# The first pair's product placed behind the scores of all four first pairs, with GpSimd's zeros put off and another order of decoding

## The chip, the cores and the metric

One core of a Trainium2 chip runs the kernel. The metric is the device time of one execution in microseconds (us), here the median of a few runs. The core has TensorE (PE in the profile, its weight loads PEld), VectorE (DVE), ScalarE (ACT), GpSimd (POOL), and SyncE (SP), which issues the transfers. Each engine works through its own list of instructions in order, and they wait for each other by semaphores.

## The reference

Windowed attention of 8 batches, 8 heads, 576 positions and 64 dimensions, then a gated network over all 4608 tokens. Heads 0 to 3 see the last 32 positions, heads 4 to 7 every fourth of the last 128.

```python
scores = scale * np.matmul(q, k.transpose(0, 1, 3, 2))
rel = pos[:, None] - pos[None, :]
mask_plain = (rel >= 0) & (rel < 32)
mask_dil = (rel >= 0) & (rel < 32 * 4) & (rel % 4 == 0)
scores = np.where(masks[None, :, :, :], scores, -1000000000.0)
attn = np.exp(scores - np.max(scores, axis=-1, keepdims=True))
attn = attn / (np.sum(attn, axis=-1, keepdims=True) + 1e-09)
x = np.matmul(attn, v)               # tokens 4608 x 512
h = x @ w_in                         # 512 x 2048
g = h * (1.0 / (1.0 + np.exp(-1.702 * h)))
out = g @ w_out                      # 2048 x 512
```

The inputs are float64; the host only rearranges and hands over their bits.

## The kernel before

**Attention.** The work is split in 32 "pairs" of heads, four to a batch (NC = 4). The first four pairs (batch 0) run in a form of their own at the start, since nothing else can be done before they give the first 512 tokens. For each: scores (two mask products at L470 with the tile ident, then 80 small products at L482 into the PSUM tile sp, which has one buffer), softmax (VectorE's maximum L502 and subtract L349, ScalarE's exponential L506, VectorE's sum L520, the added constant L510 and the reciprocal L512, GpSimd's two multiplies L349), two VectorE transposes L529 into ct (two buffers), the product with v (L575) into first_x, and the drain of first_x: ScalarE writes the high part of x (xs, L342), VectorE subtracts for the low part (xs, L349), and the rest of the tokens is copied (L342, L344). All four products write to the one tile first_x, so each waits for the drain of the one before (the key FOUR in the plan).

**Weights.** They come as 8-byte numbers and are decoded on the core. decode(n) issues one transfer of 512 KB, two scalings on ScalarE (L394, L395), the sign (L388 on ScalarE or L390 on VectorE), a shift (L398) and an add on VectorE or GpSimd, a copy for the high part (L342, L344) and a subtract for the low part (L349). n runs over w_in and w_out in turn (wi_kept, wo_kept: 16 blocks of 128 columns or rows each). The third to fifth borrow other tiles for their bits: n = 3 borrows the tile bt. bt needs zeros in it before the attention of the next batches; GpSimd writes them (L1207).

**Network.** The tokens are done in groups of 512. Groups m0 to m2 run block by block f: up products into hp (L848, 12 for each f: three for each of four c, where c is the quarter of x that pair c gives), the gate (ScalarE L856, VectorE L857, ScalarE L342 into gh and a subtract into gl), down products into acc (L785, L786, L789). The later tokens go in three blocks p, q and r that save products by sums (L991, L1106). Every product in float32 is done as three, of high and low parts.

**What sets the order.** The class Plan. Each operation is added with costs for each engine that may do it, an urgency (lower goes first), and the keys that it reads and writes; placed() then works through time and puts the operations in an order for each engine. Up to 60 us it fills TensorE's idle time with warm-up products (idle): large ones with ident (L1237) and small ones with ones (L1241). fetched() is the planner's idea of TensorE's instruction blocks: a block ends at instruction 193 and each 256 after it, and blocks holds when the next may be used. A small warm-up counts 4 instructions, a large one 2, the scores of a pair 180, a product 184.

Of the kernel before, what the change touches and what calls it, by code (L numbers as in the profile page):

```python
# [18 lines left out]
NC = DM // P  # L19
NF = DF // P  # L20
# [13 lines left out]
QT = 5  # L34
W = 64
# [12 lines left out]
class Plan:  # L48
# [62 lines left out]
    def placed(self, warm_until, soon, late=None):  # L111
# [22 lines left out]
        def fetched(count, when, cost):  # L134

            n = issued[0]
            issued[0] += count
            for j in range(len(blocks) - 1, 1 << 30):
                edge = 193 + 256 * j
                if edge >= n + count or edge > 1500:  # L140
                    return when + cost
                part = cost * (edge - n) / count
                at = max(when + part, blocks[j])
                blocks.append(at + (6.1 if at < 18.0 else 4.2))
                when, cost, n, count = at, cost - part, edge, count - (edge - n)

        open_ = [set() for _ in free]
# [4 lines left out]
        order = []  # L152
# [64 lines left out]
def tile_windowed_attention_then_gated_mlp(  # L217
# [134 lines left out]
    cells = [area(at, 2).bitcast(U64) for at in (18, 20, 4, 0, 2)]  # L352
    words = arena[:, 6:9].bitcast(U32)

    def decode(n, urgency):


# [3 lines left out]

        f = n // 2
        if n % 2:
            src, hi, lo, key = w_out[f], wo(f)[:, 0], wo(f)[:, 1], f"wo{f}"
        else:
            src, hi, lo, key = w_in[f], wi(f)[:, 0], wi(f)[:, 1], f"wi{f}"
# [42 lines left out]
    def lots(k):  # L411

        if 0 < k < NC:
            return f"first qk{k}", f"first v{k}"
        return "qk0", "v0"
# [98 lines left out]
    def softmax(k, urgency):  # L514
# [8 lines left out]
            add({POOL: 0.85, DVE: -0.48}, urgency, lambda e, a=a: pair(  # L523
                e, pr[:, a], pr[:, a], sm[:, a, :, None].broadcast_to([P, QT, W]), ALU.mult), (SM,), (f"{PR}.{a}",))
        if k < NC:

            for a in range(2):
                to = ct.rearrange("p h t a q -> p (h t a q)")[:, a * QT * W:a * QT * W + QT * W]
                add({DVE: 0.48}, urgency, lambda e, a=a, to=to: V.transpose(  # L529
                    out=to, in_=pr[:, a].rearrange("p t w -> p (t w)")), (PR, f"{PR}.{a}"), (f"{CT}.{a}",))  # L530
            return
        for half in (0, 1):
            add({DVE: 0.42}, urgency, lambda e, half=half: V.transpose(  # L533
# [145 lines left out]
        add({DMA: 66}, urgency, lambda e: load(dst, rests_x[:, y]), [f"xr{y}{i}.{n}" for i in range(NC) for n in range(3)],  # L679
            (f"tr{b}",))  # L680

    def first_attention(k, urgency):

        load_qk(k)
        load_v(k)
        add({PE: 1.5 if k else 2.3}, urgency - 1.0e5, lambda e: scores(k), (lots(k)[0],), ("sp",), count=180)
        softmax(k, urgency)
        add({PE: 1.4}, urgency - 1.0e5, lambda e: first_product(k), (lots(k)[1], f"ct{turn(k)}.0", f"ct{turn(k)}.1"), FOUR,
            count=184)
        drain_x(k, urgency)  # L690

    def attention(k, urgency):

# [501 lines left out]
              Block("r", (B, 7), (dests[B], dests[7]), late_units)]  # L1195

    for c in range(NC):
        first_attention(c, c)
        if c in (1, 2):
            decode(c - 1, c + 1.3)  # L1200
    for b, g in enumerate(main):
        g.split_x()
        if b == 0:
            for n in range(2, 2 * NF - 8):
                decode(n, 25.0 + 2.3 * n)
            zeroed = [f"bt.{m}" for m in range(8)]
            add({POOL: 1.2}, 20.0, lambda e: G.memset(bt, 0.0), (), ("bt", "btl", *zeroed))  # L1207
            add({ACT: 0.5}, 30.0, lambda e: mask_dilated(), (), ("mask",))
        if b == 1:
            for c in range(NC):  # L1210
                attention(2 * NC + c, 2000.0 + c)
            for u in range(PAIRS):
                sum_weights(u)
                sum_out_weights(u)
        if b == 2:
            for k in range(3 * NC, INNER):
                attention(k, 1000.0 * (k // NC) + k % NC)
        for f in range(NF):
            g.up(f)
            if b == 0 and f == 2:  # L1220
                for c in range(NC):
                    attention(NC + c, 46.0 + 12.9 * c)
                for n in range(2 * NF - 8, 2 * NF):
                    decode(n, 25.0 + 2.3 * n)
# [67 lines left out]
```

## Time and profile before

| | |
|---|---|
| median of 3 runs | 829.16 us (829.06 to 829.52) |
| profiled execution: its time, its span | 828.89 us, 827.2 us |
| TensorE busy in the span | 811.2 us, 98% |
| VectorE, ScalarE, GpSimd busy | 669.7 us (81%), 515.0 us (62%), 327.8 us (40%) |
| TensorE on the chain that ended last | 88% of the span |
| warm-up products in the first 38.2 us | 11.86 us |

A row of a timeline gives start and length in us, engine, line, operation, tile written and tiles read, the array's part and the shape, how many instructions are put together, and in brackets how long the engine stood idle before it and what released it. A row of a stretch gives the busy time and number of instructions of each engine in it, and the TensorE clock that was granted (1.00 is full). A wait for "issue" is one for which the profile shows no other work.

### The profile page before, as it was taken

How to read it: one execution, taken by the hardware profiler on the slowest of the kernel's cores; microseconds unless marked ns; L12 is line 12 of the kernel's file. 1: busy time of each engine (PE TensorE's matmuls, PEld its weight loads, DVE VectorE, ACT ScalarE, POOL GpSimd, SP SyncE). 2: the span in 40 equal slices, each digit the busy share in tenths (PEclk: the TensorE clock that was granted, in tenths of full speed). 3: DMA queues.
4: the chain of work that ended last, by engine and by line, in shares of the span. 5: the costliest groups of instructions: out<-in, count | busy, mean ns of one | idle time of the engine just before them, and what ended most of it. 6: DMA issues, size and time to landing. Idle time of an engine off the chain costs nothing.

```text
span 827.2 us, 18837 instructions
## 1 busy us (share of the span) xinstructions
PE 811.2 (98%) x7240; PEld 653.5 (79%) x7240; DVE 669.7 (81%) x1104; ACT 515.0 (62%) x992; POOL 327.8 (40%) x296
## 2 busy tenths in 40 slices
PE   7899999999999999999999999999999999999997
PEld 4678777888878888878788788888888888888886
DVE  6898989787888778898989998977679876867575
ACT  7998986676676777586776655446446544544340
POOL 3343336566655663324235357331125431112251
PEclk8799999999999999999999999999999999999999
DMA  9476658889757567868878878675665658664546
GB/s 359 152 244 193 181 192 287 295 281 314 249 189 254 183 200 257 267 190 280 279 229 261 261 233 260 219 269 168 214 193 182 211 186 273 203 222 149 189 151 181
DMA packets 109610, 188.12 MB, mean 227 GB/s; under 512 B 26448, under 2 KB 55376, under 8 KB 109520
## 3 DMA queue, kind: packets, MB, share of 16 engines
q1 hardware_dynamic: 109376, 186.78, 69.3%
q8 instruction: 57, 0.93, 0.5%
q14 instruction: 33, 0.27, 0.1%
q10 hardware_dynamic: 144, 0.13, 0.0%
HBM read 140.64 MB, written 45.09 MB: 225 GB/s over the span
## 4 chain that ended last, share of the span: by engine, by line
PE 88%; DVE 7%; ACT 1%; issue 1%; DMA 1%; SPq 0%; DVEq 0%; ACTq 0%
PE hp_m L848 15%; PE up_q L991 9%; PE up_r L991 9%; PE up_p L991 8%; PE second_q_Q L1106 5%; PE second_r_Q L1106 5%; PE second_p_Q L1106 5%; PE acc_m L785 5%; PE acc_m L789 5%; PE acc_m L786 4%; PE sp L482 3%; PE second_r_Z L1106 3%; PE second_R L1106 3%; PE second_q_Z L1106 3%; PE second_p_Z L1106 2%; PE av L607 2%
## 5 line engine op out<-in xcount | busy, mean ns | idle before, releaser
L349 POOL TENSOR_TENSOR arena<-arena 128x256 f32<-128x256 f32 (+3 forms) x109 | 118.0, 1091 | 155.7 <-DVE wi_last_units L349 34.7
L848 PE MATMUL hp_m<-xs,wi_kept 128*128 128x512 f32 x504 | 129.1, 398 | 0.7 <-DVE xs L349 0.4
L848 PEld LDWEIGHTS hp_m<-xs,wi_kept 128*128 128x128 f32 x504 | 93.3, 188 | 22.5 <-DVE arena L857 1.6
L342 ACT ACTIVATE wo_kept<-arena 128x512 fp32r<-128x512 f32 x115 | 71.9, 629 | 42.3 <-PE second_r_Q L1106 11.4
L349 POOL TENSOR_TENSOR wo_kept<-arena,wo_kept 128x512 fp32r<-128x512 f32 x34 | 45.3, 1340 | 105.5 <-ACT wo_kept L342 72.2
L991 PE MATMUL up_p<-wi_kept,xs 128*128 128x512 f32 x336 | 84.7, 394 | 2.2 <-DVE arena L349 1.3
L991 PE MATMUL up_r<-wi_kept,xs 128*128 128x512 f32 x336 | 85.3, 389 | 0.0
L991 PE MATMUL up_q<-wi_kept,xs 128*128 128x512 f32 x336 | 83.4, 389 | 0.0
L991 PEld LDWEIGHTS up_p<-wi_kept,xs 128*128 128x128 f32 x336 | 62.1, 188 | 16.8 <-DVE arena L349 2.2
L991 PEld LDWEIGHTS up_q<-wi_kept,xs 128*128 128x128 f32 x336 | 63.0, 188 | 13.4 <-DVE arena L1013 0.3
L991 PEld LDWEIGHTS up_r<-wi_kept,xs 128*128 128x128 f32 x336 | 63.1, 188 | 13.1
L349 DVE TENSOR_TENSOR wo_kept<-arena,wo_kept 128x512 fp32r<-128x512 f32 x87 | 65.3, 761 | 5.9 <-ACT wo_kept L342 5.4
L349 POOL TENSOR_TENSOR wo_kept<-wi_last_units,wo_kept 128x512 fp32r<-128x512 f32 x23 | 31.9, 1388 | 84.6 <-ACT wo_kept L342 84.6
L785 PE MATMUL acc_m<-gh,wo_kept 128*128 128x512 f32 x156 | 61.7, 395 | 0.4 <-ACT arena L342 0.3
L786 PE MATMUL acc_m<-gh,wo_kept 128*128 128x512 f32 x156 | 60.9, 390 | 0.0
L349 POOL TENSOR_TENSOR pr<-pr,sm 128x320 f32<-128x320 f32 x52 | 43.3, 850 | 43.0 <-DVE sm L512 29.3
L342 ACT ACTIVATE bt<-ct 32x256 f32<-32x256 f32 (+1 forms) x127 | 55.2, 435 | 3.2 <-DVE ct L533 0.9
L1012 ACT ACTIVATE arena<-arena 128x512 f32<-128x512 f32 x60 | 37.5, 628 | 28.9 <-DVE arena L349 25.1
L349 DVE TENSOR_TENSOR gl<-arena,gh 128x512 fp32r<-128x512 f32 x53 | 44.9, 847 | 9.1 <-PE acc_m L789 6.4
L349 DVE TENSOR_TENSOR arena<-arena 128x512 f32<-128x512 f32 (+1 forms) x68 | 50.4, 747 | 0.4
L1013 DVE SCALAR_TENSOR_TENSOR arena<-arena 128x512 f32<-128x512 f32 x60 | 48.1, 807 | 0.7 <-ACT arena L1012 0.2
L342 ACT ACTIVATE wo_kept<-wi_last_units 128x512 fp32r<-128x512 f32 x47 | 29.6, 629 | 30.0 <-PE second_r_Z L1106 8.9
(261 smaller groups left out, 1826.6 us busy)
## 6 DMA issues: line engine op xcount, KB each, us to landing
xs<-sums SPq DMA_DIRECT2D x168, 256.0 KB, 3.3
out_weights<-sums_o SPq DMA_DIRECT2D x63, 512.0 KB, 3.8
qk<-qk_dram SPq DMA_DIRECT2D x29, 576.0 KB, 5.2
xs<-sums_o SPq DMA_DIRECT2D x21, 512.0 KB, 3.6
v<-vp_dram SPq DMA_DIRECT2D x28, 320.0 KB, 4.4
sums<-arena SPq DMA_DIRECT2D x32, 256.0 KB, 3.6
sums_o<-arena SPq DMA_DIRECT2D x32, 256.0 KB, 3.4
arena<-wi_dram SPq DMA_DIRECT2D x15, 512.0 KB, 4.7
```

Of the source, the lines that this page charges most:

```text
L342: A.activation(dst, src, AF.Copy, scale=scale)
L349: (V if e == DVE else G).tensor_tensor(out=dst, in0=a, in1=b, op=op)
L482: T.matmul(dst[:, w:w + n], u["qk"][rows, at:at + 32], u["qk"][rows, S + first:S + first + n], start=not masked(k), stop=True, tile_positi ...
L607: T.matmul(u["x"][i][rows, at:at + last - first], u["v"][keys, a, m], bt[keys, m, a, first:last], start=(bank_, a) not in begun, stop=True ...
L785: T.matmul(self.acc[j], w[:, 0, cols], high, start=f == 0, stop=False)
L786: T.matmul(self.acc[j], w[:, 1, cols], high, start=False, stop=False)
L789: T.matmul(self.acc[j], w[:, 0, P * j:P * j + P], low, start=False, stop=f == NF - 1)
L848: T.matmul(hps[f], wi(f)[:, st, cols], mv[:, c], start=c == 0 and k == 0, stop=c == NC - 1 and k == 2)
L991: T.matmul(self.banks[place], xs[:, slot, at:at + P], wi_kept[:, 2 * a + c, mv], start=fresh and c == 0 and k == 0, stop=c == 1 and k == 2 ...
L1012: add({ACT: 0.60}, -10.0, lambda e: A.activation(unit(tmp), src(), AF.Tanh, scale=0.851), need, own(tmp))
L1013: add({DVE: -0.70 if need[0][0] == "A" else 0.70}, -10.0, lambda e: V.scalar_tensor_tensor(out=unit(dst), in0=unit(tmp), scalar=1.0, in1=s ...
L1106: T.matmul(self.second[key], w[:, st, cols], mv, start=fresh and y == 0 and k == 0, stop=y == 1 and k == 2, skip_group_check=True)
```

## The change

It has four parts. fetched() takes 4.2 us and not 6.1 for a block whose predecessor came into use before 6.0 us. The weights are decoded in another order: the second block of w_in comes ahead of the first of w_out, and the third of w_in ahead of the second of w_out; after these they alternate as before. first_attention is split in three: first_attention (loads, scores, softmax without the transposes; it now also writes a key scores0 to scores3), first_transposed (the two transposes, for pairs 2 and 3 added behind products 0 and 1) and first_multiplied (product and drain), whose product reads the key scores3, so that it follows the scores of all four pairs. And the zeros of bt get the urgency 44 in place of 20. All orders are then planned anew.

```diff
@@ -141,7 +141,7 @@
                     return when + cost
                 part = cost * (edge - n) / count
                 at = max(when + part, blocks[j])
-                blocks.append(at + (6.1 if at < 18.0 else 4.2))
+                blocks.append(at + (4.2 if at < 6.0 else 6.1 if at < 18.0 else 4.2))
                 when, cost, n, count = at, cost - part, edge, count - (edge - n)
 
         open_ = [set() for _ in free]
@@ -352,6 +352,10 @@
     cells = [area(at, 2).bitcast(U64) for at in (18, 20, 4, 0, 2)]
     words = arena[:, 6:9].bitcast(U32)
 
+
+    order = [(0, 0), (0, 1), (1, 0), (0, 2)]
+    order += [(i % 2, i // 2) for i in range(2 * NF) if (i % 2, i // 2) not in order]
+
     def decode(n, urgency):
 
 
@@ -361,8 +365,8 @@
 
 
 
-        f = n // 2
-        if n % 2:
+        out_, f = order[n]
+        if out_:
             src, hi, lo, key = w_out[f], wo(f)[:, 0], wo(f)[:, 1], f"wo{f}"
         else:
             src, hi, lo, key = w_in[f], wi(f)[:, 0], wi(f)[:, 1], f"wi{f}"
@@ -523,11 +527,6 @@
             add({POOL: 0.85, DVE: -0.48}, urgency, lambda e, a=a: pair(
                 e, pr[:, a], pr[:, a], sm[:, a, :, None].broadcast_to([P, QT, W]), ALU.mult), (SM,), (f"{PR}.{a}",))
         if k < NC:
-
-            for a in range(2):
-                to = ct.rearrange("p h t a q -> p (h t a q)")[:, a * QT * W:a * QT * W + QT * W]
-                add({DVE: 0.48}, urgency, lambda e, a=a, to=to: V.transpose(
-                    out=to, in_=pr[:, a].rearrange("p t w -> p (t w)")), (PR, f"{PR}.{a}"), (f"{CT}.{a}",))
             return
         for half in (0, 1):
             add({DVE: 0.42}, urgency, lambda e, half=half: V.transpose(
@@ -679,15 +678,28 @@
         add({DMA: 66}, urgency, lambda e: load(dst, rests_x[:, y]), [f"xr{y}{i}.{n}" for i in range(NC) for n in range(3)],
             (f"tr{b}",))
 
-    def first_attention(k, urgency):
+    def first_attention(k):
+
 
         load_qk(k)
         load_v(k)
-        add({PE: 1.5 if k else 2.3}, urgency - 1.0e5, lambda e: scores(k), (lots(k)[0],), ("sp",), count=180)
-        softmax(k, urgency)
-        add({PE: 1.4}, urgency - 1.0e5, lambda e: first_product(k), (lots(k)[1], f"ct{turn(k)}.0", f"ct{turn(k)}.1"), FOUR,
-            count=184)
-        drain_x(k, urgency)
+        add({PE: 1.5 if k else 2.3}, k - 1.0e5, lambda e: scores(k), (lots(k)[0],), ("sp", f"scores{k}"), count=180)
+        softmax(k, k)
+
+    def first_transposed(k):
+        y = turn(k)
+        pr, ct = prs[y], cts[y].rearrange("p h t a q -> p (h t a q)").rearrange("p (a n) -> p a n", a=2)
+        for a in range(2):
+            add({DVE: 0.48}, k, lambda e, a=a: V.transpose(
+                out=ct[:, a, 0:QT * W], in_=pr[:, a].rearrange("p t w -> p (t w)")), (f"pr{y}", f"pr{y}.{a}"), (f"ct{y}.{a}",))
+
+    def first_multiplied(k):
+
+        y = turn(k)
+        add({PE: 1.4}, k - 1.0e5, lambda e: first_product(k), (lots(k)[1], f"ct{y}.0", f"ct{y}.1", f"scores{NC - 1}"),
+            FOUR, count=184)
+        drain_x(k, k)
 
     def attention(k, urgency):
 
@@ -1195,16 +1207,22 @@
               Block("r", (B, 7), (dests[B], dests[7]), late_units)]
 
     for c in range(NC):
-        first_attention(c, c)
+        first_attention(c)
+        if c < 2:
+            first_transposed(c)
         if c in (1, 2):
             decode(c - 1, c + 1.3)
+    for c in range(NC):
+        first_multiplied(c)
+        if c < 2:
+            first_transposed(c + 2)
     for b, g in enumerate(main):
         g.split_x()
         if b == 0:
             for n in range(2, 2 * NF - 8):
                 decode(n, 25.0 + 2.3 * n)
             zeroed = [f"bt.{m}" for m in range(8)]
-            add({POOL: 1.2}, 20.0, lambda e: G.memset(bt, 0.0), (), ("bt", "btl", *zeroed))
+            add({POOL: 1.2}, 44.0, lambda e: G.memset(bt, 0.0), (), ("bt", "btl", *zeroed))
             add({ACT: 0.5}, 30.0, lambda e: mask_dilated(), (), ("mask",))
         if b == 1:
             for c in range(NC):
```

TensorE between the scores of pair 0 (sp_187) and of pair 1 (sp_250 before, sp_264 now), before:

```order
L482 MATMUL sp_187<-qk_126 32x16
L1237 LDWEIGHTS ident
L1237 MATMUL idle<-ident 128x512
...
L1237 MATMUL idle<-ident 128x512
L470 LDWEIGHTS ident
L470 MATMUL sp_250<-plain,ident 128x320
L482 MATMUL sp_250<-arena 32x64 x35
```

and now:

```order
L486 MATMUL sp_187<-qk_126 32x16
L1259 MATMUL idle<-ones 32x16 x19
L1255 LDWEIGHTS ident
L1255 MATMUL idle<-ident 128x512
L1255 LDWEIGHTS ident
L1255 MATMUL idle<-ident 128x512
L474 LDWEIGHTS ident
L474 MATMUL sp_264<-plain,ident 128x320
L474 LDWEIGHTS ident
```

Where seven large warm-ups stood (two rows each, five of them left out above), there are 19 small ones and two large.

TensorE from the scores of pair 2 (sp_320) to the product of pair 1 (which reads ct_92), before; sp_439 are the scores of pair 3:

```order
L482 MATMUL sp_320<-arena 32x16
L575 MATMUL first_x<-ct_91,v_129 64x32 x6
L575 MATMUL first_x<-ct_91,v_129 64x64 x24
...
L1237 LDWEIGHTS ident
L1237 MATMUL idle<-ident 128x512
...
L482 MATMUL sp_439<-arena 32x64 x35
...
L482 MATMUL sp_439<-arena 32x16
L575 MATMUL first_x<-ct_92,arena 64x32 x6
L575 MATMUL first_x<-ct_92,arena 64x64 x24
```

and now, from the scores of pair 3 (sp_406) on; nine large warm-ups stand between the scores of pairs 2 and 3:

```order
L486 MATMUL sp_406<-arena 32x64 x35
...
L486 MATMUL sp_406<-arena 32x16
L574 MATMUL first_x<-ct_91,v_129 64x32 x6
L574 MATMUL first_x<-ct_91,v_129 64x64 x24
...
L1255 LDWEIGHTS ident
L1255 MATMUL idle<-ident 128x512
...
L1255 MATMUL idle<-ident 128x512
L574 MATMUL first_x<-ct_92,arena 64x32 x6
L574 MATMUL first_x<-ct_92,arena 64x64 x24
```

The product of pair 0 (it reads ct_91 and v_129) has moved from ahead of the scores of pair 3 to behind them, and seven large warm-ups follow it before the product of pair 1.

VectorE from the reciprocal of pair 1 on (mx_85 and sm_88 are the maximum and sum of pair 2, mx_86 is the maximum of pairs 1 and 3), before:

```order
L512 RECIPROCAL sm_89<-sm_89 128x10
L502 TENSOR_REDUCE mx_85<-sp_320 128x10
L344 COPY arena<-first_x 128x64
L349 TENSOR_TENSOR pr_83<-sp_320,mx_85 128x640
L349 TENSOR_TENSOR xs<-first_x,xs 128x432
L349 TENSOR_TENSOR xs<-first_x,xs 128x80
L529 STREAM_TRANSPOSE ct_92<-pr_84 128x320 x2
L520 TENSOR_REDUCE sm_88<-pr_83 128x10
L510 TENSOR_SCALAR sm_88<-sm_88 128x10
L512 RECIPROCAL sm_88<-sm_88 128x10
```

and now, from the maximum of pair 2 on:

```order
L506 TENSOR_REDUCE mx_85<-sp_334 128x10
L514 TENSOR_SCALAR sm_89<-sm_89 128x10
L349 TENSOR_TENSOR pr_83<-sp_334,mx_85 128x640
L516 RECIPROCAL sm_89<-sm_89 128x10
L349 TENSOR_TENSOR wi_kept<-arena,wi_kept 128x512
L524 TENSOR_REDUCE sm_88<-pr_83 128x10
L693 STREAM_TRANSPOSE ct_92<-pr_84 128x320
L514 TENSOR_SCALAR sm_88<-sm_88 128x10
L693 STREAM_TRANSPOSE ct_92<-pr_84 128x320
L516 RECIPROCAL sm_88<-sm_88 128x10
L506 TENSOR_REDUCE mx_86<-sp_406 128x10
L349 TENSOR_TENSOR pr_84<-sp_406,mx_86 128x640
```

The drain of product 0 (the copy of first_x and the xs rows) stood inside the softmax of pair 2; now it comes behind the maximum and subtract of pair 3, and a subtract for the second block of w_in stands there. On ScalarE the read of the first hp for the gate (L856, now L868) stood behind three decoding steps that follow the last xs copy, and stands behind five now.

## The prediction

> **What bounds the kernel now.** I read the stretches first, to find where TensorE is not full, then its waits, then the timelines of the start. Columns of the stretches: length, busy time and instructions of TensorE, its weight loads, VectorE, ScalarE and GpSimd, then the granted TensorE clock, DMA share, GB/s.
>
> ```profile
> 0.00:38.20 38.20, 30.32 (x837) 19.18 (x837) 27.52 (x64) 31.16 (x44) 14.82 (x23) 0.82 0.67 250
> 38.20:340.00 301.80, 300.99 (x3689) 241.51 (x3690) 256.80 (x450) 226.60 (x472) 152.86 (x154) 1.00 0.74 239
> ...
> PE up_p L991 <- DVE arena L349: 1.3, 2, 0.7
> PE up_p L991 <- DVE arena L1013: 0.9, 1, 0.9
> PE hp_m L848 <- DVE xs L349: 0.4, 1, 0.4
> PE acc_m L785 <- ACT arena L342: 0.3, 1, 0.3
> PE second_r_Q L1106 <- DMA out_weights<-sums_o: 0.2, 1, 0.2
> PE hp_m L848 <- DVE arena L857: 0.2, 1, 0.2
> ```
>
> After 38.2 us TensorE is bound by its own work: the wait rows (us in total, times, longest) after that time add up to 3.3 us. So the change acts on the start: TensorE's instructions are the same work afterwards, and what counts is when the first down product (acc) begins, at 41.94 us, by which both orders have done the same 36 up products. TensorE's timeline up to there (start, us, engine, line, tiles, partitions and shape, count, wait before):
>
> ```profile
> 6.44 3.14 PE L1237 MATMUL idle<-ident 128*128 128x512 bf16 x7
> 9.40 0.45 PE L470 MATMUL sp<-plain,ident 128*128 128x320 bf16 x2
> ...
> 10.79 2.12 PE L1237 MATMUL idle<-ident 128*128 128x512 bf16 x9
> 13.06 0.43 PE L470 MATMUL sp<-arena,ident 128*128 128x320 bf16 x2 [0.15 <-DVE pr L349]
> ...
> 16.02 0.40 PE L482 MATMUL sp<-arena 64*32 64x64 f32 x21 [1.76 <-issue]
> ...
> 19.62 0.71 PE L470 MATMUL sp<-arena,ident 128*128 128x320 bf16 x2 [0.23 <-DVE pr L349]
> ...
> 22.31 1.37 PE L482 MATMUL sp<-arena 64*32 64x64 f32 x75 [1.60 <-issue]
> ...
> 25.70 0.91 PE L575 MATMUL first_x<-ct,arena 32*64 32x64 f32 x39 [0.90 <-issue]
> 26.54 1.65 PE L848 MATMUL hp_m<-xs,wi_kept 128*128 128x512 f32 x3
> ...
> 29.42 1.23 PE L575 MATMUL first_x<-ct,arena 32*64 32x64 f32 x80
> ...
> 34.00 1.08 PE L575 MATMUL first_x<-ct,arena 32*64 32x64 f32 x80
> ...
> 38.18 3.92 PE L848 MATMUL hp_m<-xs,wi_kept 128*128 128x512 f32 x16 [0.43 <-DVE xs L349]
> 41.94 0.39 PE L785 MATMUL acc_m<-gh,wo_kept 128*128 128x512 f32 x1
> ```
>
> Three waits are for "issue", that is for nothing the profile shows. The planner's own model explains their places: instruction blocks end at instruction 193 and every 256 after it (193, 449, 705, 961, 1217), a small warm-up counts 4, a large one 2, scores 180, a product 184. Counted so, the stalls sit where block ends 705 (scores 2), 961 (scores 3) and 1217 (product 1) fall. The first two stalls end 6.29 us apart (16.02, 22.31), the next 3.39 later. I read this as: a block is usable about 6.3 us after the one before came into use while DMA is full, 3.4 when it is quiet.
>
> The second thing the start shows is the clock (same columns as above; the cuts are where it can change):
>
> ```profile
> 6.00:9.43 3.43, 3.43 (x47) 1.42 (x29) 2.39 (x4) 2.94 (x4) 0.00 (x0) 1.00 1.02 410
> 9.43:12.84 3.41, 3.41 (x96) 1.87 (x94) 3.22 (x8) 2.66 (x5) 0.51 (x1) 1.00 1.02 416
> 12.84:16.26 3.42, 1.51 (x87) 1.05 (x86) 2.10 (x6) 3.32 (x6) 2.33 (x3) 1.00 1.01 405
> 16.26:19.67 3.41, 3.19 (x117) 1.94 (x100) 2.30 (x8) 2.93 (x5) 2.64 (x3) 0.50 1.03 410
> 19.67:23.10 3.43, 1.83 (x69) 1.07 (x75) 3.36 (x9) 3.43 (x7) 0.76 (x2) 0.50 0.75 292
> 26.50:29.90 3.40, 3.40 (x42) 1.64 (x39) 3.30 (x7) 3.05 (x7) 2.42 (x3) 0.50 0.82 272
> 29.90:38.20 8.30, 7.87 (x177) 5.32 (x162) 6.06 (x14) 7.25 (x9) 2.81 (x3) 1.00 0.19 59
> ```
>
> The seven large warm-ups from 6.44 take 0.427 us each until the clock comes up near 9.43, and nine take 2.12 at full clock (0.216 each, 0.24 with gaps). A stretch full of large matmuls is followed by full clock; one with 1.51 busy of 3.42 (12.84 to 16.26) by half; one 93% busy, but with only some 43% of it large warm-ups (16.26 to 19.67), did not raise it.
>
> **The change part by part.**
> *Warm-ups between scores 0 and 1.* Seven large ones become 19 small and two large. The small ones take 4 instructions each, so block end 449 is passed before scores 1 and not inside it. Scores 1 was waiting only for those warm-ups; its probabilities' subtract is done at 9.02 by this row, so it may begin at 9.2 in place of 9.40.
>
> ```profile
> 8.20 0.82 DVE L349 TENSOR_TENSOR pr<-sp,mx 128x640 f32<-128x640 f32 x1
> 18.61 0.23 DVE L344 COPY arena<-first_x 128x64 f32<-128x64 f32 x1 [1.11 <-ACT xs L342]
> 25.60 0.49 DVE L529 STREAM_TRANSPOSE ct<-pr 128x320 f32<-128x320 f32 x1
> 27.45 0.76 DVE L349 TENSOR_TENSOR xs<-first_x,xs 128x432 fp32r<-128x432 f32 x2
> 28.12 1.20 DVE L510 TENSOR_SCALAR sm<-sm 128x10 f32<-128x10 f32 x1
> 35.11 1.09 ACT L342 ACTIVATE xs<-first_x 128x512 fp32r<-128x512 f32 x1
> 38.31 0.68 ACT L394 ACTIVATE arena<-arena 128x512 f32<-128x512 f32 x1 [0.38 <-POOL wi_kept L349]
> 38.88 0.59 ACT L856 ACTIVATE arena<-hp_m 128x512 f32<-128x512 f32 x1
> 41.02 0.62 ACT L342 ACTIVATE gh<-arena 128x512 fp32r<-128x512 f32 x1
> 41.54 1.35 ACT L388 ACTIVATE arena<-arena 128x512 f16<-128x512 f32 x1
> 26.72 0.90 POOL L1207 MEMSET bt<- 128x960 f32 x1 [1.54 <-DVE arena L349]
> 28.01 1.28 POOL L349 TENSOR_TENSOR wi_kept<-arena,wi_kept 128x512 fp32r<-128x512 f32 x1 [0.40 <-ACT wi_kept L342]
> ```
>
> But the stretch 6.0 to 9.43 now holds two large warm-ups, 0.85 us, beside small work: 25% where it was 88%. By the rows it should leave the clock at half, so scores 1 takes about 2.1 us (scores 3, at half: mask 0.71, and 1.37 for 75 of 84 records, a little overlapped) and ends at 11.3, and the nine large warm-ups behind it take 3.84 in place of 2.12, up to 15.1. Scores 2 therefore begins at 15.1, 2.0 us later than now. The bounds for the clock's return are 9.4 (no loss at all) and 29.9 (where it returns now). Between, I count large work by stretch: 9.43 to 12.84 holds 46% large warm-ups, nearest to the 43% that did not raise it; 12.84 to 16.26 holds 67% and a mask product besides. I take 16.3.
>
> *Product 0 behind scores 3.* With block end 449 passed near 8 us and product 0 no longer ahead, 705 lies 51 instructions into scores 2 and is passed at 16.1 without a stall (now: 1.76). Scores 2 ends at 16.9. Scores 3 waits for the softmax of pair 2, which took 3.2 us behind scores 2 now; 1.3 of that was VectorE standing for the drain of product 0 (the copy at 18.61 and the 1.11 before it), which is out of the way. With 1.95 for nine warm-ups at full clock, scores 3 begins at 18.9. Block end 961 lies 109 instructions into it, passed at 20.0, usable at 16.1 + 6.3 = 22.4: the stall moves, and grows to 2.4. Product 0 then starts at 22.8, where the trace has 16.35; product 1, now at 23.61, cannot start until product 0's result is drained from the same tile: product 1.2, drain 1.7 (now 26.54 to 28.21, the two xs subtracts), so 25.7 at best. Seven large warm-ups stand between them. After a stretch with little more than a microsecond of work in it (19.67 to 23.1) I expect half clock once more, and they last until 26.8.
>
> *Products 1 to 3.* These stand behind each other by the drain. Product 1 takes 1.0; six up products at full clock (0.24 each from 16 in 3.92) and four warm-ups end at 30.1, and the drain with a transpose or two in it (0.49 each) at 30.3: product 2 at 30.3 (now 29.42). From product 2 to 3 I take the trace's own 4.58 (29.42 to 34.00), since the same kind of drain and decoding stands there: 34.9, with 0.3 for a third transpose 35.2.
>
> *From product 3 to the first down product.* TensorE has less to do here now: nine up products behind the last drain, not 16. What ends last is the gate: ScalarE reads hp0 only behind five decoding steps that are queued ahead. Its xs copy ends 2.2 us after product 3 starts (34.00 to 36.20), the steps take 4.0 (four like the 0.68 of L394 and one of 1.35), the gate's read 0.59, VectorE's product some 0.7 by its neighbours, another weight's copy and the gate's own 0.62 each: 8.9 with 0.2 of gaps, so acc at 44.1. That is 2.2 us later than 41.94. The bounds are the case without that queue (8.0, as in the trace: 34.00 to 41.94), and the same at a clock that never falls, the rivals below.
>
> *Order of decoding and GpSimd's zeros.* The second w_in block comes before the first w_out block, and the third into bt. SP issues the same transfers of the same sizes, and each q/k load keeps its place among them, so I cost the queue at nothing; were one q/k load later, the next scores would wait as long. hp1 gets its weights earlier, acc later: three subtracts for w_out now stand on GpSimd behind the fourth pair's multiplies, 1.28 each, so some 4 us, and end near 37 if they begin where product 2 does plus a drain, before acc needs them. The zeros (0.90 us of GpSimd) move behind the fourth pair's multiplies. Gain there: the sum's add-constant at 28.12 took 1.20 while GpSimd worked; at most 1.0 us off pair 3's softmax, but now this softmax is covered by three waiting products, so I cost it at nothing; without that cover it would be 1.0 in favour.
>
> *The rest of the plan.* Every later instruction order is made anew, with the same work. The gain is bounded by the 3.3 us of waits; the two rows of up_p on VectorE (2.2) are decoding that came too late, and they shrink when TensorE comes 2.2 later: I take 0.8 off, since decoding in the start is shifted with the drains too. As a loss I allow the same 1.5 us or so.
>
> Sum: +2.2 - 0.8 = +1.4 us. The profiled execution took 828.89, so it would take 830.3; the median of the runs is 0.27 higher, 829.16, and with it 830.6.
>
> On the clock's fall the Trainium skill ("TensorE: Matmul & The Clock Gate", the table of Why this matters for your kernels) states that a whole window of idle, some 3 us, takes the clock back to half. The trace differs: it was at half from 16.26 behind a single gap of 1.76 us. By that rule the fourth rival below would hold.
>
> **The rivals.**
> *The clock keeps full from 9.4 or 12.8 (faster, or no change).* Then scores 2 stays at 13.06 (VectorE sets it), its 1.76 us stall is gone, scores 3 is at 18.0 and resumes at 13.8 + 6.3 = 20.1; product 0 at 20.5, 2.3 earlier than above, product 1 at 23.6 and acc at 40.8 to 42: -1.1 to 0, so 828.0 to 829.2. For it: 9.43 to 12.84 would be all busy with 46% of large warm-ups, and the trace kept full clock with 62% (2.12 of 3.41); against it: the 25% ahead of 9.43, and the 43% that did not raise it. It decides if the rows show 1.00 from 9.43 or 12.84.
> *Half until 29.9 (slower).* If 67% of large warm-ups do not raise it either, scores 3 ends at 23.1, seven warm-ups of 0.427 behind product 0 put product 1 at 27.4, six up products at half (1.65 for three now) end past 31, product 2 at 31.7, acc at 45: +3.0, less 0.8: 831.4, and 832.2 if nothing is given back. For it: 16.26 to 29.90 at half now.
> *The later plan decides.* Decoding is just in time after 42 us, and a weight that comes sooner or later moves more than the start does: up to -3.3 with every wait gone (825.9, or 827 with the late start), or +1.5 on top of the sum (832.1).
> *The clock stays full through the stall in scores 3.* If a gap of 2.4 us does not lower it, the seven warm-ups fit into the drain, product 1 starts at 25.7 and acc comes 1.1 earlier, at 43.0: 829.5. For it: nothing in these rows; against it: the half clock behind the 1.76 us gap. The page on the clock gate, named above, speaks for it.
> *The change does nothing to the stalls.* If a block's latency counts from its transfer and not from the block before, the stall in scores 3 ends near 20 as in the first rival, at half clock: +0.3, so 829.5.
>
> By the Trainium skill ("Runtime: NRT & Kernel Launch", Instruction fetch mechanics) the crossing into a next block of 256 instructions is mostly hidden; here it costs 1.76, 1.60 and 0.90 us, so I go by the rows.
>
> **How the numbers follow.** 0.2% (1.66 us) is about what a measurement of this kernel can tell from no change: faster means under 827.5, slower over 830.8. Forecast (half clock to 16.3 and again to 26.5): 0.36, with 1 us either way from the later plan: same 0.20, slower 0.15, faster 0.01. Full clock kept: 0.20, same 0.13, faster 0.07. Half until 29.9: 0.15, slower. Later plan decides: 0.16, faster 0.13, slower 0.03. Full through the stall: 0.08, same. Stalls alone: 0.05, same. Sums: faster 0.21, same 0.46, slower 0.33. The range reaches from the kept clock with a microsecond gained later, 827.0, to half clock until 29.9 with nothing given back, 832.4.
>
> **What would show it.** Right: granted clock 0.50 behind 9.43, scores 2 near 15.1, one stall of over 2 us in scores 3 and none in scores 2, product 0 near 22.8, acc near 44. Wrong: clock 1.00 from 9.43 on, product 0 before 21; or acc at 44 and yet the same or a shorter time, with the up_p waits gone, which would mean that the supply of weights, not the start, sets the end.

## The result: 835.75 us, slower by 0.78%, and the profile after

The changed kernel takes 835.75 us in the median of six runs (833.6 to 837.4), the kernel before 829.14 (828.83 to 829.65). The ratio is 1.0078, with a 95% interval of 1.0064 to 1.0093. The profiled execution took 836.09 us, with a span of 834.4; the one of before took 828.89, so there are 7.2 us to be found.

TensorE's timeline of the changed kernel up to the first down product comes first (start, us, engine, line, tiles, partitions and shape, count, wait before it):

```profile
7.06 0.61 PE L1255 MATMUL idle<-ident 128*128 128x512 bf16 x1
8.29 0.59 PE L1255 MATMUL idle<-ident 128*128 128x512 bf16 x1 [0.62 <-issue]
9.04 0.71 PE L474 MATMUL sp<-plain,ident 128*128 128x320 bf16 x2 [0.17 <-DVE pr L349]
9.69 1.45 PE L486 MATMUL sp<-arena 64*32 64x64 f32 x84
11.06 2.36 PE L1255 MATMUL idle<-ident 128*128 128x512 bf16 x9
13.26 0.43 PE L474 MATMUL sp<-arena,ident 128*128 128x320 bf16 x2
...
14.72 0.78 PE L486 MATMUL sp<-arena 64*32 64x64 f32 x54 [0.64 <-issue]
...
20.91 0.38 PE L486 MATMUL sp<-arena 64*32 64x64 f32 x21 [2.02 <-issue]
21.23 1.36 PE L574 MATMUL first_x<-ct,v 32*64 32x32 f32 x92
22.52 3.01 PE L1255 MATMUL idle<-ident 128*128 128x512 bf16 x7
25.47 1.16 PE L574 MATMUL first_x<-ct,arena 32*64 32x32 f32 x92
...
33.47 1.08 PE L574 MATMUL first_x<-ct,arena 32*64 32x64 f32 x80 [0.90 <-DVE xs L349]
...
41.79 0.50 PE L797 MATMUL acc_m<-gh,wo_kept 128*128 128x512 f32 x1 [1.57 <-ACT gh L342]
```

The first down product starts at 41.79 us, where it started at 41.94 before. In these two executions the new start loses nothing. So all of the 7.2 us lies behind it, where both kernels do the same work in another order.

From the first up product of block q on, TensorE does the same products in the same order in both kernels, but for one exchange near 500 us, so the rows can be laid side by side. Before, then now:

```profile
486.58 0.84 PE L991 MATMUL up_q<-wi_kept,xs 128*128 128x512 f32 x3
...
496.79 1.52 PE L1106 MATMUL second_p_Q<-wo_kept,out_weights 128*128 128x512 f32 x6
...
509.70 1.52 PE L1106 MATMUL second_p_Q<-wo_kept,out_weights 128*128 128x512 f32 x6
...
488.55 0.84 PE L1003 MATMUL up_q<-wi_kept,xs 128*128 128x512 f32 x3
...
501.82 1.84 PE L1118 MATMUL second_p_Q<-wo_kept,out_weights 128*128 128x512 f32 x6 [2.49 <-DVE wi_last_units L1139]
...
516.48 1.52 PE L1118 MATMUL second_p_Q<-wo_kept,out_weights 128*128 128x512 f32 x6
```

The changed kernel is 2.0 us behind at the first of these rows, 5.0 at the second, 6.8 at the third and 7.2 at the end. So 2.1 us are lost between the first down product and block q, 4.8 at the turn from block p to block q, and 0.4 behind it. TensorE's waits over the whole execution of the changed kernel (us in total, times, longest) name the places:

```profile
PE sp L486 <- issue: 2.7, 2, 2.0
PE second_p_Q L1118 <- DVE wi_last_units L1139: 2.5, 1, 2.5
PE hp_m L860 <- DVE arena L869: 2.0, 4, 0.8
PE acc_m L797 <- ACT gh L342: 1.8, 2, 1.6
...
PE second_p_R L1118 <- DMA out_weights<-sums_o: 0.9, 1, 0.9
...
PE av L606 <- ACT arena L342: 0.8, 1, 0.8
...
PE second_q_Z L1118 <- DMA xs<-sums_o: 0.5, 1, 0.5
PE sp L486 <- DMA qk<-qk_dram: 0.4, 1, 0.4
```

All but the first row add up to 8.9 us; 1.6 of that is the wait that ends with the first down product at 41.79. So 7.3 us lie behind the first down product, where the kernel before had 2.9 (the prediction's 3.3 without the 0.4 ahead of 41.94). The 2.2 us of up products in block p (L991, waiting for VectorE) are gone, as the prediction hoped, and others have come in their place. The longest, 2.5 us, stands at the turn from block p to block q. TensorE's timeline there, and two stretches of it (length, then busy time and instructions of TensorE, its loads, VectorE, ScalarE, GpSimd; granted clock; DMA share; GB/s):

```profile
496.45 1.52 PE L1118 MATMUL second_p_Q<-wo_kept,xs 128*128 128x512 f32 x6
...
503.45 5.03 PE L1003 MATMUL up_q<-wi_kept,xs 128*128 128x512 f32 x15
...
503.00:504.00 1.00, 1.00 (x5) 0.78 (x4) 1.00 (x2) 0.73 (x2) 0.00 (x0) 0.56 0.92 350
506.00:506.50 0.50, 0.50 (x3) 0.39 (x2) 0.50 (x2) 0.00 (x0) 0.00 (x0) 0.50 0.98 119
```

In this execution the wait costs twice: behind it the clock fell to half, and 15 up products took 5.03 us where 15 at full clock take 3.57 (a row of an experiment, below). With the six products ahead of them, 1.84 against 1.52, the half clock adds about 1.8, so the wait and the clock cost some 4.3 of the 7.2 us here. The wait's cause is read from VectorE's timeline ahead of it:

```profile
489.42 1.79 DVE L349 TENSOR_TENSOR wi_kept<-ct,wi_kept 128x512 fp32r<-128x512 f32 x1
491.13 1.78 DVE L349 TENSOR_TENSOR wo_kept<-wi_last_units,wo_kept 128x512 fp32r<-128x512 f32 x1
...
494.03 1.83 DVE L349 TENSOR_TENSOR wi_last_units<-wi_last_units,arena 128x512 f32<-128x512 f32 x1
495.79 1.77 DVE L349 TENSOR_TENSOR wo_kept<-arena,wo_kept 128x512 fp32r<-128x512 f32 x1
...
500.49 0.68 DVE L349 TENSOR_TENSOR wi_kept<-pr,wi_kept 128x512 fp32r<-128x512 f32 x1
501.09 1.27 DVE L1139 SCALAR_TENSOR_TENSOR wi_last_units<-second_p_Q,wi_last_units 128x512 f32<-128x512 f32 x2
...
489.29 1.36 POOL L349 TENSOR_TENSOR wi_kept<-qk_units,wi_kept 128x512 fp32r<-128x512 f32 x1 [4.96 <-ACT wi_kept L342]
490.86 1.50 POOL L349 TENSOR_TENSOR wi_kept<-pr,wi_kept 128x512 fp32r<-128x512 f32 x1 [0.20 <-ACT wi_kept L342]
492.32 1.74 POOL L349 TENSOR_TENSOR wi_kept<-v_units,wi_kept 128x512 fp32r<-128x512 f32 x1
494.01 1.30 POOL L349 TENSOR_TENSOR gl<-arena,gh 128x512 fp32r<-128x512 f32 x1
495.39 1.62 POOL L349 TENSOR_TENSOR arena<-arena 128x512 f32<-128x512 f32 x1
```

VectorE is busy without a gap, and four of its elementwise operations of L349 (subtracts and sums), which take 0.68 us where GpSimd stands still, take 1.77 to 1.83 while GpSimd works beside them: 4.5 us more. The adds that empty the PSUM tiles for which TensorE waits come at 501.09, as the last of that queue, 3.1 us behind the products that they read (496.45 and 1.52). In the kernel before the same two adds follow these products at once, at 495.59 (the products: 494.06 and 1.52), and only one such operation in that stretch takes as long:

```profile
490.28 1.78 DVE L349 TENSOR_TENSOR wi_last_units<-wi_last_units,arena 128x512 f32<-128x512 f32 x1
...
495.59 1.28 DVE L1127 SCALAR_TENSOR_TENSOR wi_last_units<-second_p_Q,wi_last_units 128x512 f32<-128x512 f32 x2
```

### The profile page after: what moved, and what is told of

Read it like the earlier page. It is cut to its first block, busy times and chain, and to the rows that moved or that the text cites. A ratio compares the mean times of both kernels' runs of the same rounds, so it can differ in the third digit from the quotient of the medians.

```text
span 834.4 us, 18931 instructions
## 1 busy us (share of the span) xinstructions
PE 813.3 (97%) x7283; PEld 653.9 (78%) x7283; DVE 681.0 (82%) x1121; ACT 515.0 (62%) x986; POOL 314.6 (38%) x285
## 5 line engine op out<-in xcount | busy, mean ns | idle before, releaser
L349 POOL TENSOR_TENSOR arena<-arena 128x256 f32<-128x256 f32 (+3 forms) x98 | 104.7, 1077 | 133.1 <-DVE wi_last_units L349 26.0
L349 POOL TENSOR_TENSOR wo_kept<-arena,wo_kept 128x512 fp32r<-128x512 f32 x39 | 54.2, 1396 | 131.0 <-ACT wo_kept L342 84.8
L349 POOL TENSOR_TENSOR pr<-pr,sm 128x320 f32<-128x320 f32 x52 | 41.1, 806 | 80.7 <-DVE sm L516 64.2
L349 DVE TENSOR_TENSOR wo_kept<-arena,wo_kept 128x512 fp32r<-128x512 f32 x82 | 64.3, 792 | 7.9 <-ACT wo_kept L342 7.1
L349 POOL TENSOR_TENSOR wo_kept<-wi_last_units,wo_kept 128x512 fp32r<-128x512 f32 x20 | 26.9, 1343 | 76.5 <-ACT wo_kept L342 73.4
L349 DVE TENSOR_TENSOR arena<-arena 128x512 f32<-128x512 f32 (+1 forms) x74 | 54.4, 737 | 0.5
L349 DVE TENSOR_TENSOR gl<-arena,gh 128x512 fp32r<-128x512 f32 x52 | 41.9, 805 | 4.9 <-PE acc_m L801 2.4
```

Of the source, the lines that this page charges most:

```text
L349: (V if e == DVE else G).tensor_tensor(out=dst, in0=a, in1=b, op=op)
```

## The experiments

All times are medians, all ratios are to the kernel before in runs of the same time on the same chip (829.18 to 829.36 us), with 95% intervals. What is read from a trace is read from one execution of each kernel.

| kernel | us | ratio |
|---|---|---|
| new start, old rest | 829.58 | 1.0005 (0.9996 to 1.0014) |
| old start, new rest | 835.59 | 1.0076 (1.0059 to 1.0092) |
| new to 335 us, then old | 834.76 | 1.0062 (1.0046 to 1.0079) |
| old to 335 us, then new | 837.77 | 1.0097 (1.0076 to 1.0118) |
| moved product alone | 828.07 | 0.9983 (0.9974 to 0.9992) |
| all but the moved product | 830.00 | 1.0013 (1.0001 to 1.0025) |
| new to 470 us, then old | 833.11 | 1.0048 (1.0035 to 1.0060) |
| old to 470 us, then new | 831.51 | 1.0026 (1.0014 to 1.0037) |
| new start, old rest, gate first | 829.92 | 1.0006 (0.9997 to 1.0014) |
| adds first | 835.20 | 1.0077 (1.0064 to 1.0090) |
| old, due times from 125 us | 828.25 | 0.9995 (0.9985 to 1.0006) |
| new start, rest of moved product | 828.95 | 1.0003 (0.9993 to 1.0014) |
| old start, rest of moved product | 828.81 | 1.0001 (0.9989 to 1.0012) |
| new order, old engines | 833.02 | 1.0048 (1.0033 to 1.0063) |
| old order, new engines | 828.73 | 0.9993 (0.9984 to 1.0003) |
| new, old engines in 470 to 520 us | 833.83 | 1.0050 (1.0033 to 1.0067) |

**Start or rest.** Both kernels have the same 4215 operations, so one plan's order can be continued with the other's. The planner is left out and a fixed table gives the order and the engine of each. The diffs of this section are shortened; where an order is a table in the run, a comment says what it holds:

```diff
-        order, starts = self.placed(warm_until, soon)
-        for _ in range(ROUNDS):
-            order, starts = self.placed(warm_until, soon, self.latest(starts, SINCE))
+        order = TABLE   # changed plan up to 60 us of its own time, then what is left, as the plan before has it
```

> The new order of every engine up to 60 us of planned time, and from there the order that the kernel before has, as a fixed table. Theory (the loss sits in the later order, since the first down product came at 41.79 us in the changed kernel and at 41.94 before): within 1 us of before, 828.5 to 830, first down product near 41.8. Rival (the new start hands the later part a supply of weights that costs it time whatever its order): 833 or more, with the losses behind 340 us again.

> The old order up to 60 us planned, then the changed kernel's later order. Theory (later order): 833 to 837, the change's own time, with a wait of TensorE of 2 us or more near 495 to 502. Rival (the start costs it): 829 to 831.

The rest decides, and the start hardly anything: 829.58 with the new start, 835.59 with the new rest behind the old start, which is the change's whole loss. The traces agree: the first down product comes between 41.5 and 43.4 us in the eight kernels with the new start, and between 41.4 and 43.8 in the seven with the old one. The old start with the new rest shows the same wait as the changed kernel, and the new start with the old rest the waits of the kernel before, besides the gate's of 1.56 at the end of the start. First the former's waits behind 340 us, then the latter's:

```profile
PE second_p_Q L1204 <- DVE wi_last_units L1225: 2.5, 1, 2.5
...
PE up_p L1101 <- DVE arena L447: 1.3, 2, 0.7
PE up_p L1101 <- DVE arena L1123: 0.9, 1, 0.9
```

**Where in the rest.** The same tables, cut at 335 us:

```diff
-        order = TABLE   # cut at 60 us
+        order = TABLE   # cut at 335 us, new then old; and old then new
```

> The changed kernel's order up to 335 us planned, then the order of before. The up products of the plain groups end at 338.66 us before and 338.90 in the changed kernel, so by the theory that the loss is made in the order behind that point (block p and the turn to q): 829 to 831. Rival (what was put off before 335 us, the down products and the decoding, costs it later in any order): 833 to 837.

> The old order up to 335 us planned, then the changed kernel's. If the order behind 335 us costs by itself: 832 to 837. If the loss needs both the new first part and the new second part: 828.5 to 830.5.

Both are slow, the first against what I expected, so this cut tells nothing of the place. The two plans stand at different points there: in the changed plan the down products of the last plain group run until 382 us, in the old one until 366. Joined at 335 us, one has work left that the other's order does not reckon with; that this is what costs was not tested. The old-then-new kernel shows a wait that neither plan has by itself:

```profile
PE up_p L1089 <- DVE arena L955: 3.6, 1, 3.6
```

At 470 us the plans are at the same point in this respect, and there the cut works:

> The changed kernel's order up to 470 us planned, then that of before. The changed kernel lost 4.4 us in one place at 499 to 507 us: a wait of 2.5 and then 15 products of which the first eight ran at half clock. Theory (VectorE's work of 489 to 497, slowed beside GpSimd's, makes that wait): with the old order there the wait is gone or under 0.5 us, and the time 830.5 to 832. Rival (VectorE is late by what came before 470): the wait stays, 834 to 837.

> The order of before up to 470 us planned, then the changed kernel's. If the stretch behind 470 is bad by itself (the wait of 2.5 us and the half clock): 832 to 834. Rival (VectorE comes late into it): 829 to 830.5, with a wait under 1 us there.

The order before 470 costs 0.48% and the order behind it 0.26%, 4.0 and 2.2 us. That is some 6.1 together, against 6.3 to 6.6 for all. Neither expectation was met whole. With the new order up to 470, and the old one behind it, the long wait is gone, as I expected: TensorE goes on at 501.37 without one. But the time was not 830.5 to 832, and a wait of 1.0 us stands 13 us earlier, for adds on another tile, where neither plan has one by itself. So up to 1.0 of the 4.0 us belongs to the joint. With the old order up to 470 the long wait is there, but at 1.4 us, and the clock holds. The first two rows are from the former kernel's timeline, the others from the latter's:

```profile
488.31 1.65 PE L1216 MATMUL second_p_Q<-wo_kept,out_weights 128*128 128x512 f32 x6 [1.01 <-DVE arena L1237]
...
501.37 1.65 PE L1216 MATMUL second_p_Q<-wo_kept,out_weights 128*128 128x512 f32 x6
...
500.35 1.66 PE L1204 MATMUL second_p_Q<-wo_kept,out_weights 128*128 128x512 f32 x6 [1.38 <-DVE wi_last_units L1225]
501.85 3.57 PE L1089 MATMUL up_q<-wi_kept,xs 128*128 128x512 f32 x15
```

**Which part of the change.** The diff taken apart: the product's move alone (first_attention, first_transposed, first_multiplied and their loops), and the rest of the diff without it (block times, decoding order, zeros).

```diff
-        first_attention(c, c)
+        first_attention(c)   # and first_transposed, first_multiplied as in the change; order and zeros as before
```

> The kernel before with the split of the first attention alone: all four products behind the scores; the block times, the order of decoding and the zeros as before. Its plan gives 210 operations behind 60 us to another engine than before. Theory (what costs is the plan anew behind the start, and the moved product sets it off): 833 to 837. Rival (the decoding order or the zeros set it off): 828.5 to 830.5.

> The changed kernel with the products where they stood before: block times, decoding order and zeros changed. Its plan gives 25 operations behind 60 us to another engine, all of them before 130 us. Theory: 828.5 to 830, no change. Rival (decoding order): 833 or more.

My theory fell here. The moved product alone sets off as large a new plan as the whole change (210 operations on another engine behind 60 us; the change has 196), and it is faster than before by 0.17%, the only kernel that is faster clear of noise. Without it the change costs 0.13%, with 25 operations on another engine. Neither of these two parts has the loss. The other combinations of the diff's parts were not run, so it is open whether all of them are needed for it. Whether the gain of the moved product sits in its rest was tried with tables again:

```diff
+        order = TABLE   # new start, or old start, up to 60 us; then the order of the moved product alone
```

> The changed kernel's start (up to 60 us planned), then the order of the kernel with the moved product alone, which ran in 828.07. If the rest sets the time: 827.5 to 829. If that gain came from its own start: 829 to 830.5.

> The old start, then the order of the kernel with the moved product alone. If its gain (1.2 us) came from the rest, where the waits of the sums in block p (2.2 us) are gone: 827.5 to 828.8. If it came from the start (first down product 0.3 us earlier) or needs it: 829 to 830.5.

Neither start gains with that rest (1.0003 and 1.0001); the times of 828.95 and 828.81 lie where the two expectations meet. Where the gain of 0.17% sits was not settled.

**Is a new plan as such dangerous?** One number of the planner, the time from which it goes by due times, and the start as it was:

```diff
-ROUNDS, SINCE, CALM, ROOM = 3, 130.0, 8.0, 3.0
+ROUNDS, SINCE, CALM, ROOM = 3, 125.0, 8.0, 3.0
```

> The kernel before with one number of the planner changed: it goes by its due times from 125 us planned, not from 130. The start is the same, 197 operations go to another engine behind 125 us, as many as by the change. If a plan made anew costs or gains by chance: beyond 0.2% from before, either way (under 827.6 or over 830.9). Rival (a plan made anew is worth the same, and only one that starts from the moved products is bad or good): 828.6 to 829.9.

The rival held: 0.9995. The two other new plans as large as the changed kernel's (this one and the moved product's), and the smaller one of all but the product, are off by 0.17% at most; the changed kernel's is off by 0.78%. Four plans are too few to say how often one turns out so.

**Order or engine.** The changed plan gives GpSimd fewer elementwise operations and VectorE more; the first parts of the pages, before and after:

```profile
PE 811.2 (98%) x7240; PEld 653.5 (79%) x7240; DVE 669.7 (81%) x1104; ACT 515.0 (62%) x992; POOL 327.8 (40%) x296
...
PE 813.3 (97%) x7283; PEld 653.9 (78%) x7283; DVE 681.0 (82%) x1121; ACT 515.0 (62%) x986; POOL 314.6 (38%) x285
```

Two kernels exchange only the engine of the 104 operations that moved between the two, in either order. Another 92 operations moved between VectorE and ScalarE; these stay where the order has them, so "order" here takes them in:

```diff
+        order = [(i, other[i]) if {e, other[i]} == {DVE, POOL} else (i, e) for i, e in order]   # behind 60 us
```

> The changed kernel's order, but the 104 operations behind 60 us planned that went from VectorE to GpSimd or back (57 to VectorE, 47 to GpSimd) are on the engine that they have in the kernel before. If VectorE's load is the cause: 829 to 832. Rival (the order in time is): 834 to 838.

> The order of before, with those 104 operations on the engine that the changed kernel gives them. If VectorE's load is the cause: 832 to 836. Rival (the order in time): 828.5 to 830.5. An operation in a place planned for the other engine can cost by itself, which raises both.

The load of VectorE is not the cause by itself: the old order bears the new engines (0.9993), though its trace has the long wait too, at 1.2 us; it came to that place 1.4 us earlier than the kernel before. The new order with the old engines is at 1.0048, between the two expectations, so in that order the choice between VectorE and GpSimd is worth some 2.5 us, and the order in time, with the 92 others, the other 4. The same exchange in the stretch of the long wait alone, 19 operations:

> The changed kernel with the operations of 470 to 520 us planned that it moved between VectorE and GpSimd on their old engine. If their engines make the wait at 499: it falls under 1 us and the time to 832 to 833.5. Rival: the wait stays at 2 us or more, 835 to 836.5.

The wait fell from 2.5 to 0.5 us and the clock held (the 15 products took 3.57 us). The time is 833.83, a little above the 832 to 833.5 expected and some 1.9 below the changed kernel's, though the ends of the two intervals (1.0067 and 1.0064) still meet. That is less than half of the 4.3 us that the wait and the clock cost in the changed kernel's trace. Its wait:

```profile
PE second_p_Q L1216 <- DVE wi_last_units L1237: 0.5, 1, 0.5
```

**Two waits taken away by order alone.** In the changed kernel three subtracts were put behind the adds that end the long wait. In the kernel with new start and old rest, the first gate was put ahead of other work: on ScalarE its read ahead of a decoding step and its high copy ahead of a weight's, on VectorE its product ahead of a copy and a shift.

```diff
-  DVE: wo_kept, (wi_kept), wi_last_units, wi_kept subtracts; then the two adds of second_p_Q
+  DVE: (wi_kept) subtract; the two adds of second_p_Q; then the other three subtracts
```

> The changed kernel's order, but for VectorE near 499 us: three subtracts (0.6 us each) that stood ahead of the two adds of second_p_Q, for which TensorE waited 2.5 us, come behind them. If that wait and the half clock behind it are the 4.4 us lost there: the wait falls to 0.7 or less, the clock stays full, and the time falls by 1.8 to 3.7, to 832.0 to 834.0. Rival (VectorE is full, and the time comes back at the next wait): 835 to 836.5.

> New start and old rest, and in the start the first gate (ScalarE's read of hp0, VectorE's product and the high copy) is put ahead of one decoding step on each engine. With new start and old rest TensorE waited 1.56 us for that gate at 42.28. If that wait is worth its length: it falls to about 0.8, and the time by 0.5 to 1.0, to 828.3 to 829.0. Rival (decoding behind it is late by as much and the time comes back): 829.2 to 829.6.

Both rivals held. The long wait fell to 0.7, a wait of 1.2 for VectorE's L447 (the helper that is L349 in the changed kernel) came 5 us later, and the time stayed (1.0077). In its trace the turn itself took 1.9 us less than in the changed kernel's, since the clock held. But 1.0 us more was lost ahead of it, in the same order, and 1.5 behind it, where the changed kernel lost 0.4; two waits for transfers of out_weights took 2.1 us in this execution. So the wait that came back is only part of why the time stayed. The gate's wait of 1.56 went away, and the time stayed (1.0006); up products waited 0.8 for VectorE instead. Rows of the two kernels, in that order:

```profile
PE second_p_Q L1216 <- DVE wi_last_units L1237: 0.7, 1, 0.7
PE up_q L1101 <- DVE arena L447: 1.2, 1, 1.2
...
PE hp_m L958 <- DVE arena L967: 0.8, 2, 0.6
```

What stays open: why the order between 60 and 470 us costs 4 us. The traces show 2.1 us of it in the changed kernel, between the first down product and block q, and 2.1 to 2.7 in all five kernels that have this order (this one, old start with new rest, new to 470 without the wait at the joint, adds first, and old engines in 470 to 520). TensorE's waits there add up to 4.3 us in the changed kernel (2.0 in four for VectorE's product of the gate, 0.9 and 0.4 for transfers, 0.8 for a copy, 0.2 for a gate), against 2.7 before. None is over 0.9 us, and no single one was shown to carry the loss.

## Why the prediction was wrong

The forecast was 830.6 us (827.0 to 832.4), no change; measured were 835.75. The step that failed is the last term of the sum, "the rest of the plan": I put it at -0.8 us, with 1.5 us as the largest loss, and it was +6.3 (old start, new rest). The 3.3 us of waits in the trace before bound what a new order can gain. They say nothing about what it can lose, and I took the bound of the gain for one of the loss without a row for it. What the runs showed in its place: 2.1 us in a new order up to block q, and 4.8 at the turn to it, where VectorE, slowed beside GpSimd, emptied two PSUM tiles 3.1 us late and the clock fell behind the wait. VectorE at 256.80 of 301.80 us could have warned me that a loss was possible, but it does not tell a bad plan from a good one: between 60 and 510 us the kernel with due times from 125 us has more of VectorE's work than the changed one (392.64 against 390.83 us), and is not slower. The rival "The later plan decides" came nearest. It put the loss in the later plan, but gave late weights as the reason, where the waits shown are most of all for VectorE's adds and the gate's product, and a price of 1.5 us where it was four times that.

The start's term was too large as well, +2.2 us: with the new start and the old rest the kernel took 0.3 us more than before, which is no change. The upper end of the range, 832.4, is also 0.2 above its own sum (829.16 and 3.0).

The start, on which most of the working was spent, went point by point in the profiled execution:
- Scores 1 at 9.2 and at half clock: 9.04, and its 84 records took 1.45 us, as scores 0 did at half. Right.
- Clock back at 16.3, scores 2 at 15.1: wrong. The nine warm-ups from 11.06 took 2.2 us up to 13.26, which is full clock for most of them, so it was back between 11 and 12, and scores 2 came at 13.26. Up to then only two large warm-ups had run, with small ones and the scores of two pairs beside them; I had counted only large work. The rival of the kept clock was the nearest.
- No stall in scores 2: 0.64 us. One of over 2 us in scores 3: 2.02. From the one block to the next it took 6.19 us (14.72 to 20.91), as worked out from the rows before (6.29). Right but for the small one, and for one of 0.62 among the warm-ups ahead of scores 1.
- Half clock again behind that stall: right, with some luck. Seven warm-ups from 22.52 took 3.01 us, 0.43 each. By the rule of the Trainium skill ("TensorE: Matmul & The Clock Gate", Why this matters for your kernels) a pause of 2.02 us should have left it full; the trace disagrees here as it did before. But in the kernel with the new start and the rest of the moved product the same stall, of 1.76 us there, left the clock full, and the seven warm-ups took 1.69.
- Product 0 at 22.8, product 1 at 26.8, acc at 44.1: 21.23, 25.47 and 41.79. The error of 1.6 in product 0 is the clock's. From product 3 to acc it took 8.3 us against 8.9, with the wait for the gate behind ScalarE's decoding steps in its place (1.57).

With the start right, the sum would have been the rival's, 828.0 to 829.2; the kernel with the new start and the old rest took 829.58, just above that.

## What to carry to other kernels

Where a planner sets the whole order, a change to the first 40 us is a change to everything behind it. The waits of the trace bound what a new order can win; its loss has to be looked for in the new order itself, where an engine that is nearly full feeds the bound one. To judge the edit apart from the new plan behind it, fix that order by a table: here the edit was worth 0.05%, which is no change (0.9996 to 1.0014), and the later plan 0.76%. Do not add up what waits cost in one trace and expect it back: two kernels in which the long wait was taken away by order, or shortened by another engine, gave back nothing and 1.9 us of 4.3.

## What the runs showed of the hardware

- A pause of TensorE of 2.49 us in the middle of full work took the clock to half for about 3.4 us (granted 0.56 in 503 to 504, 0.50 at 506 to 506.5), which cost 1.8 us more; behind pauses of 1.38 and 1.21 us the products went on at full speed.
- The length of the pause alone does not decide. In the kernel with the moved product alone a pause of 2.26 us (20.42 to 22.68) left the clock full: eight warm-ups behind it took 1.90 us. In the two traces the recorded changes of the clock stand whole multiples of 3.41 us apart. Cut into such stretches, the changed kernel's pause at 499.3 lies all but 0.4 us in one, in which TensorE was busy for 1.30 us, and half clock follows; the other's is divided between two, busy for 2.42 and 2.13, and full clock follows. The rows are of the first and of the last of these stretches:

```profile
499.71:503.12 3.41, 1.30 (x6) 1.09 (x7) 3.41 (x7) 0.00 (x0) 0.00 (x0) 1.00 0.61 204
...
21.40:24.81 3.41, 2.13 (x85) 1.51 (x86) 2.16 (x5) 2.46 (x5) 1.24 (x2) 1.00 0.30 118
```

- The granted clock reads 1.00 in the first 9 us of both kernels, while large warm-ups took 0.43 us each there in the kernel before and 0.22 later, and the 84 records of scores 1 took 1.45 us in the changed one at 9.69, where they took 1.07 before: ahead of its first change the column is no evidence, the durations are.
- VectorE's elementwise operations of L349 on 128x512 took 0.68 us where GpSimd stood still, and four of them 1.77 to 1.83 beside GpSimd's elementwise work between 489 and 498 us. In the changed kernel's whole trace none that reads SBUF alone and had no GpSimd work beside it took over 0.72.
